# Near units of a block-sparse attention: key slots as row groups of the scores, squares turned on VectorE, sums from a column of ones

## The chip, the core and the metric

The kernel runs on one core of a Trainium2 chip. A core has five engines that work side by side: TensorE (PE, matrix products into PSUM), VectorE (DVE), ScalarE (ACT), GpSimd (POOL) and SyncE (SP, which here only issues transfers). The metric is the time of one execution in microseconds (us), the median of several runs.

## The reference

Two layers follow each other: a block-sparse attention and a channel mix.

```python
batch, n_heads, seq, head_dim = (4, 8, 768, 64); block = 32; n_rand = 3
mask = |blk_i - blk_j| <= 1  or  blk_i, blk_j in (0, 23)     # 24 blocks of 32 rows
mask[rows of qb, columns of kb] = True   for kb in sampled_blocks[qb]   # 3 drawn
scores = where(mask, q k^T / 8, -1e9)
attn = exp(scores - max); attn /= sum(attn) + 1e-9
x = (attn v), heads side by side                       # (4, 768, 512)

x_prev = x one row earlier (zeros ahead of row 0)
xk = mu_k x + (1 - mu_k) x_prev;  xr likewise with mu_r
out = sigmoid(xr w_r) * ((relu(xk w_k) ** 2) w_v)      # w_k 512x1024, w_v 1024x512, w_r 512x512
```

## The kernel before

The attention is cut into 24 units of 128 query rows, six for each batch b. Unit (b, 0) is a wide one: blocks 21, 22, 23 and 0, whose rows look at all or nearly all 24 blocks. The units (b, 1) to (b, 5) are near units: four blocks each (QB = 4), and each block looks at eight key slots of 32 keys: block 0, block 23, its own block and both neighbours, and three drawn blocks. `UNITS` puts the wide ones early: (0,0), (1,0), (2,0), (0,1), (0,2), (3,0), then the other near units in order.

A near unit is worked by `near_group`, twice, four heads at a time. Scores `s` are 16 products (L524) of 32 query rows by 256 keys, with a pair of heads in the two halves of the rows and the four blocks in the four column groups of the array, so the partitions of `s` are the query rows. VectorE adds the mask and takes the row's extreme in one operation a head (`soft`, L479); ScalarE takes the exponential with that as bias and sums the row into `L` (`exp`, L489); `turn` transposes 128x128 squares on PE into PSUM `t` (L500), and VectorE copies them back to `pt` (L506); 32 products of 64 columns with the values in VR make `o` (L546). `finish` divides `o` by `L` (L609), transposes the unit's `x` (`tx`, L606) and ScalarE puts it into `xt`, the input of the mixer.

The keys of a near unit lie in four buffers of KR (of five), one for each block with its eight slots: SP loads the three neighbours from kd, the ends once a batch, and the drawn blocks from kt, by numbers read from a register. The values of a block lie in one of six buffers VR: SP loads the known 128 rows (vw), GpSimd gathers the others by a list of rows (vt).

The channel mix goes by windows of 256 rows: `gate` (r, L713), `hidden` (h_0p to h_3p, L731) and `values` (v, L760), three products with numbers split in two parts for each product of the reference. A window needs the near units that cover its rows, so mixer and attention run side by side on PE; the windows of the last batch come after the attention.

All operations are first recorded by `Plan.add`, each with its engine, a cost in ns, a rank (its due time), what it reads and writes, and a release time. `Plan.order` then lists them engine by engine; what it lists is the program's order on each engine. The constants behind the functions (due times such as O_MAX and O_PV, lead times such as LEAD_K, M_STEP of the mixer, numbers of buffers) set this order. PSUM's eight banks stand as: `t` two, `m` (mixer) one, `o` one, `s` two of two banks each.

Of the kernel before, what the change touches and what calls it, by code (L numbers as in the profile page):

```python
# [18 lines left out]
P = 128  # L19
# [10 lines left out]
QB, NC, SLOTS = 4, 5, 8  # L30
# [185 lines left out]
def block_sparse_attention_channel_mix(  # L216
# [24 lines left out]
    KR = [fixed([P, SLOTS, HP * BLK], F32, f"KR{i}") for i in range(KR_BUFS)]  # L241
    VR = [fixed([P, 2, DM], F32, f"VR{i}") for i in range(VR_BUFS)]
    number = fixed([1, NB * NRAND * 2], I32, "number")
# [3 lines left out]
    near_mask = fixed([P, NC, SLOTS], F32, "near_mask")  # L247
# [6 lines left out]
    def mask_setup():  # L254
        own = buf([P, NC + 1, NRAND, 2], I32, "kk", 3, "own")
        con = buf([P, NC * (SEEN + SLOTS) + 2 * NB + 2], F32, "zr", 3, "con")
        pick = buf([P, NC * QB, 2], I32, "kk", 3, "pick")
        f = buf([P, NC + 1, NRAND], F32, "dif", 2, "ownf")
        same = buf([P, NB * NRAND], F32, "x0", 1, "same")
        word = buf([P, 2 * NB], F32, "x1", 1, "word")  # L260
        line = buf([P, NC * QB], F32, "pt", PT_BUFS, "line")
        near = NC * SEEN
        stat = near + NC * SLOTS
        plan.add(SP, ISSUE, -30, lambda: nc.sync.dma_start(number.ap, blocks), writes=[(number,)], size=2000)
        plan.add(ACT, ISSUE, -32, lambda: nc.scalar.dma_start(own.ap.rearrange("p a b c -> p (a b c)"), rows), writes=[(own,)], size=20000)
        plan.add(ACT, ISSUE, -31, lambda: nc.scalar.dma_start(con.ap, consts), writes=[(con,)], size=60000)
        plan.add(ACT, ISSUE, PICK, lambda: nc.scalar.dma_start(pick.ap.rearrange("p a b -> p (a b)"), picks), writes=[(pick,)], size=20000)
# [12 lines left out]
        def find():  # L280
            v = nc.gpsimd
            c = con.ap
            v.tensor_copy(out=line.ap, in_=pick.ap[:, :, 0])
# [8 lines left out]
        def far():  # L292
            v = nc.vector
            v.tensor_copy(out=f.ap, in_=own.ap[:, :, :, 0])
            c = con.ap

            e = same.ap.rearrange("p (a b) -> p a b", b=NRAND)
            v.tensor_tensor(
                out=e, in0=c[:, stat : stat + NB].unsqueeze(2).to_broadcast([P, NB, NRAND]),
                in1=f.ap[:, 0, :].unsqueeze(1).to_broadcast([P, NB, NRAND]), op=ALU.is_equal)  # L300
            v.tensor_reduce(out=wide_mask.ap, in_=e, axis=AX.X, op=ALU.max)
            v.tensor_tensor(out=wide_mask.ap, in0=wide_mask.ap, in1=c[:, stat + NB : stat + 2 * NB], op=ALU.max)
            v.tensor_scalar(out=wide_mask.ap, in0=wide_mask.ap, scalar1=1.0, scalar2=FAR, op0=ALU.subtract, op1=ALU.mult)

        def twice():
            v = nc.vector
            c = con.ap
            v.tensor_copy(out=near_mask.ap, in_=c[:, near:stat].rearrange("p (a b) -> p a b", b=SLOTS))
            g = f.ap[:, 1:, :]
            e = same.ap[:, 0 : NRAND * SEEN].rearrange("p (a b) -> p a b", b=SEEN)  # L310
            for a in range(NC):
                v.tensor_tensor(
                    out=e, in0=g[:, a, :].unsqueeze(2).to_broadcast([P, NRAND, SEEN]),
                    in1=c[:, a * SEEN : (a + 1) * SEEN].unsqueeze(1).to_broadcast([P, NRAND, SEEN]), op=ALU.is_equal)
                v.tensor_reduce(out=near_mask.ap[:, a, SEEN:], in_=e, axis=AX.X, op=ALU.max)
# [104 lines left out]
    def load_unit(b, u, at):  # L420
# [7 lines left out]
        if u == 0:  # L428
# [484 lines left out]
```

## Time and profile before

| what | value |
|---|---|
| timed runs | 616.49, 617.76, 619.31 us; median 617.76 |
| span of the profiled execution | 616.1 us (its time is given by this span alone) |
| PE, weight loads of PE | 575.8 us (93%), 465.5 us (76%) |
| DVE, ACT, POOL | 303.8 (49%), 300.6 (49%), 344.0 (56%) |
| transfers | 114.18 MB, mean 185 GB/s |

The span is that of the slowest core, of which there is one. PE's busy time is the time in which at least one product was in work; products overlap, and their ends are modelled, so in a list by time the distance from one start to the next tells more than the lengths. The rows that follow in the prediction are of three kinds: a table by stretch of time, a list of one engine by time, and groups by line of the kernel.

### The profile page before, as it was taken

The page shows a single profiled execution, that of the slowest core. Times are in us where ns is not written, and L with a number is a line of the kernel's source. Part 1 is how long each engine was busy: PE and PEld are TensorE (multiplying, and loading weights), DVE is VectorE, ACT ScalarE, POOL GpSimd, SP SyncE. Part 2 cuts the span into 40 slices and gives each one's busy share as a digit, 9 for nine tenths or more (in the row PEclk, how much of TensorE's full clock was granted, in tenths as well). Part 3 has the DMA queues.
Part 4 walks back from the last instruction along what each step waited for, and adds up shares of the span by engine and source line. Part 5 has one row for each costly group of instructions (what it writes and reads, how often), then busy time and mean ns, then how long its engine had stood idle before and what let it go on. Part 6 is the DMA issues. An engine that isn't in the chain of part 4 may idle for free.

```text
span 616.1 us, 20666 instructions
## 1 busy us (share of the span) xinstructions
PE 575.8 (93%) x8172; PEld 465.5 (76%) x8172; DVE 303.8 (49%) x906; ACT 300.6 (49%) x712; POOL 344.0 (56%) x400
## 2 busy tenths in 40 slices
PE   8887878798899999999999989999999999999997
PEld 3564655587667878878788778778778788989897
DVE  6677768873864255264443452653632532423300
ACT  3675845583544545355535534635545454333341
POOL 1324344865777737657836835546467464664551
PEclk9999989999899999999999999999999999999999
DMA  8959659858786667766764774774666620000001
GB/s 310 399 157 379 231 168 335 282 164 286 219 261 217 188 193 212 210 181 202 227 200 164 232 227 146 233 229 147 224 188 182 201 75 1 36 18 18 17 18 35
DMA packets 88499, 114.18 MB, mean 185 GB/s; under 512 B 12626, under 2 KB 59219, under 8 KB 88403
## 3 DMA queue, kind: packets, MB, share of 16 engines
q1 hardware_dynamic: 81570, 91.79, 46.7%
q0 software_dynamic: 6400, 20.98, 10.7%
q8 instruction: 65, 1.06, 0.7%
q10 hardware_dynamic: 432, 0.10, 0.2%
q14 instruction: 32, 0.25, 0.1%
HBM read 106.01 MB, written 6.82 MB: 183 GB/s over the span
## 4 chain that ended last, share of the span: by engine, by line
PE 63%; DVE 10%; ACT 8%; issue 6%; POOL 5%; DMA 3%; another core or an unknown queue 2%; SPq 2%; ACTq 0%; DVEq 0%; POOLq 0%
PE v L760 17%; PE o L546 5%; PE h_1p L731 5%; PE h_3p L731 5%; PE r_0p L713 5%; PE t L500 5%; PE r_1p L713 4%; PE h_2p L731 4%; ACT p L489 4%; PE s L524 3%; PE h_0p L731 2%; PE tw L500 2%; PE sw L563 2%; PE o L585 2%
## 5 line engine op out<-in xcount | busy, mean ns | idle before, releaser
L760 PE MATMUL v<-wv,k 128*128 128x512 f32 (+1 forms) x600 | 139.4, 386 | 1.4 <-DVE z L768 1.4
L760 PEld LDWEIGHTS v<-wv,k 128*128 128x128 f32 x600 | 107.5, 188 | 26.5 <-DVE xr_2f L680 2.1
L489 ACT ACTIVATE p<-p,nm 128x256 f32<-128x256 f32 x160 | 79.4, 498 | 48.7 <-DVE nm L479 48.7
L470 POOL DMA_INDIRECT VR<-vt,lines x80 | 79.0, 988 | 33.1 <-PE o L546 16.0
L506 DVE COPY pt<-t 128x512 f32<-128x512 f32 x80 | 53.0, 686 | 81.5 <-PE t L500 74.6
L479 DVE CUSTOM_DVE_ANT_1 p<-s,near_mask 128x256 f32<-128x256 f32 x160 | 57.9, 418 | 30.4 <-remote 19.4
L689 POOL TENSOR_TENSOR xr<-xr_1f,xr 128x256 fp32r<-128x256 f32 x24 | 17.7, 740 | 72.0 <-ACT xr L687 71.9
L524 PE MATMUL s<-KR,q 64*32 64x256 f32 x1280 | 50.8, 381 | 1.0 <-PE tw L500 0.9
L500 PE MATMUL t<-ident,p 128*128 128x128 f32 x320 | 47.5, 283 | 3.8 <-ACT p L489 2.3
L546 PEld LDWEIGHTS o<-VR,pt 128*32 128x32 f32 x2560 | 37.9, 110 | 15.0 <-issue 8.8
L546 PE MATMUL o<-VR,pt 128*32 128x64 f32 x2560 | 44.7, 221 | 2.3 <-issue 1.4
L687 ACT CAST xr<-xr_1f 128x256 fp32r<-128x256 f32 x24 | 9.7, 405 | 72.9 <-PE r_0p L713 43.0
L731 PE MATMUL h_1p<-xk,wk 128*128 128x256 f32 x288 | 37.0, 283 | 8.2 <-ACT h_0k L744 4.6
L609 DVE TENSOR_TENSOR x<-o,R 128x512 f32<-128x512 f32 x24 | 16.6, 691 | 56.8 <-PE o L546 53.7
L500 PEld LDWEIGHTS t<-ident,p 128*128 128x128 f32 x320 | 36.9, 144 | 9.3 <-ACT p L489 6.4
L731 PEld LDWEIGHTS h_1p<-xk,wk 128*128 128x128 f32 x288 | 34.7, 188 | 10.3 <-ACT h_0k L744 5.5
L731 PEld LDWEIGHTS h_0p<-xk,wk 128*128 128x128 f32 x288 | 34.9, 188 | 3.6 <-issue 3.3
L713 PE MATMUL r_1p<-wr,xr 128*128 128x512 f32 x144 | 37.7, 411 | 0.0
L524 PEld LDWEIGHTS s<-KR,q 64*32 64x32 f32 x1280 | 27.1, 105 | 13.8 <-issue 3.8
L731 PE MATMUL h_3p<-xk,wk 128*128 128x256 f32 x288 | 36.8, 282 | 0.4 <-ACT h_2k L744 0.4
L731 PEld LDWEIGHTS h_2p<-xk,wk 128*128 128x128 f32 x288 | 34.6, 188 | 3.3 <-ACT k L745 3.3
L731 PE MATMUL h_0p<-xk,wk 128*128 128x256 f32 x288 | 36.9, 283 | 0.0
(115 smaller groups left out, 1043.7 us busy)
## 6 DMA issues: line engine op xcount, KB each, us to landing
VR<-vw SPq DMA_DIRECT2D x80, 256.0 KB
KR<-kd SPq DMA_DIRECT2D x80, 192.0 KB
KR<-kt SPq DMA_DIRECT2D x240, 64.0 KB
k_ring<-kq SPq DMA_DIRECT2D x16, 384.0 KB
VR<-vt SPq DMA_DIRECT2D x24, 256.0 KB
q<-qt SPq DMA_DIRECT2D x23, 256.0 KB
out<-z SPq DMA_DIRECT2D x23, 256.0 KB
early_w<-w_k SPq DMA_DIRECT2D x8, 512.0 KB
```

The costliest lines, as they stand in the source:

```text
L470: plan.add(POOL, GATHER, at - LEAD_V + 0.01 * j, lambda w=w, n=n: nc.gpsimd.indirect_dma_start(VR[w].ap[:, 1, :], None, vt.rearrange("b n ...
L479: nc.vector.tensor_tensor_reduce(out=p.ap[:, cs].rearrange("p (a x) -> p a x", x=BLK), in0=view().rearrange("p (a x) -> p a x", x=BLK), in ...
L489: plan.add(ACT, 280 + 0.83 * (cs.stop - cs.start), rank, lambda: nc.scalar.activation(p.ap[:, cs], p.ap[:, cs], AF.Exp, bias=nm.ap[:, col ...
L500: nc.tensor.transpose(tp.ap[:, i, :], p.ap[:, cs], ident.ap)
L506: plan.add(DVE, 600, rank + 0.1, lambda: nc.vector.tensor_copy(out=pt.ap, in_=tp.ap), reads=[(tp,)], writes=[(pt,)])
L524: nc.tensor.matmul(s.ap[ROWS[j], row, a * 256 : (a + 1) * 256].rearrange("p (n x) -> p n x", x=BLK), q.ap[half, hp, ROWS[j]], KR[keys[j]]. ...
L546: nc.tensor.matmul(o.ap[ROWS[j], h * D : (h + 1) * D], pts[i // 2].ap[:, 2 * (i % 2) + g, ROWS[j]], VR[values[j]].ap[:, g, h * D : (h + 1) ...
L609: plan.add(DVE, 600, rank, lambda: nc.vector.tensor_tensor(out=x.ap.rearrange("p (h d) -> p h d", d=D), in0=o.ap.rearrange("p (h d) -> p h ...
L689: plan.add(POOL, 80 + 2.4 * MIX * tw, rank + O_MIX, lambda f=f, cs=cs: nc.gpsimd.tensor_tensor(out=dst.ap[:, 1, cs], in0=f.ap, in1=dst.ap[ ...
L713: nc.tensor.matmul(pr.ap[:, 0:512], xr.ap[:, a, c, :], wr.ap[:, w, c, :], start=(c == 0 and m == 0), stop=(c == CC - 1 and m == 2))
L731: nc.tensor.matmul(ph.ap[:, ff * TT : (ff + 1) * TT], wk.ap[:, w, c, f * P : (f + 1) * P], xk.ap[:, a, c, :], start=(c == 0 and m == 0), s ...
L760: nc.tensor.matmul(pv.ap[:, 0:width], k2.ap[:, a, f, i * P : (i + 1) * P], wv.ap[:, w, f, cs], start=(f == 0 and m == 0), stop=(f == FC - ...
```

## The change

`near_unit` takes the place of `near_group` and works all eight heads of a unit. The partitions of `s` were the 128 query rows; now row group i of `s` holds slot pair i for the 32 rows of a block, and the four blocks lie side by side in the columns: a product (L536) takes 32 query rows and the 64 keys of one slot pair. A row of queries so has its 256 scores on four partitions, 64 on each. The maximum is then taken in three steps: over 64 keys by VectorE (`tops`), from row group to row group by 16 products with parts of the unit matrix (`G`), over the four by VectorE again (`base`, with the penalty for slots that stand twice). VectorE subtracts (L567), ScalarE takes the exponential of 1024 columns without a sum, VectorE turns every 32x32 square in place (L572), and the products with the values read that directly: the key slots are already the rows. V has a 65th column of ones for each head, so the sum of a row comes out in `o`; `o` is two halves of one bank each, and `finish` divides each half for itself. PE's transposes of `p` go for near units; the wide units keep theirs.

KR becomes two buffers of a whole unit (6 neighbouring blocks, the two ends, 12 drawn). In PSUM, `t` and `m` become one tag of two banks, `o` gets two. The mask setup changes with it, and all of the planner's costs and due times have new numbers.

```diff
-QB, NC, SLOTS = 4, 5, 8
+QB, NC = 4, 5
+END, DRAWN = QB + 2, QB + 4
+KEYS = DRAWN + QB * NRAND
+DV = D + 1
+HD = H * DV
...
-    KR = [fixed([P, SLOTS, HP * BLK], F32, f"KR{i}") for i in range(KR_BUFS)]
-    VR = [fixed([P, 2, DM], F32, f"VR{i}") for i in range(VR_BUFS)]
+    KR = [fixed([P, KEYS, HP * BLK], F32, f"KR{i}") for i in range(KR_BUFS)]
+    VR = [fixed([P, 2, HD], F32, f"VR{i}") for i in range(VR_BUFS)]
...
+        plan.add(SP, ISSUE, at_k, lambda: nc.sync.dma_start(
+            KR[r].ap[:, 0:END].rearrange("p n x -> p (n x)"), kd[b, :, n0 - 1 : n0 + QB + 1].rearrange("p n x -> p (n x)")),
+            writes=[(KR[r], "near")], release=at_k, size=65536 * END)
...
                 for i in range(NRAND):
+                    nc.sync.dma_start(KR[r].ap[:, DRAWN + NRAND * j + i, :],
+                                      kt[bass.ds(sampled_block(n0 + j, i) + b * NB, 1)].rearrange("o p x -> p (o x)"))
...
-        tp = buf([P, 4, P], F32, "t", T_BUFS, f"t{name}", ps)
+        tp = buf([P, 4, P], F32, "m", M_BUFS, f"t{name}", ps)
...
+    def near_unit(b, u, q, keys, values, o, t0, gap):
...
+        G = buf([P, QB, 2 * C], F32, "m", M_BUFS, f"G{name}", ps)
+        for gi in range(2):
...
+            def mm(s=s, gi=gi):
+                for a in range(2):
+                    hp = 2 * gi + a
+                    for j in range(QB):
+                        for i in range(QB):
...
+                            for row, half in enumerate(HALF):
+                                at = (a * QB + j) * 2 * BLK
+                                nc.tensor.matmul(
+                                    s.ap[ROWS[i], row, at : at + 2 * BLK].rearrange("p (n x) -> p n x", x=BLK),
+                                    q.ap[half, hp, ROWS[j]], KR[keys].ap[half, near : far + 1 : far - near, hp * BLK : (hp + 1) * BLK],
+                                    start=True, stop=True, skip_group_check=True)
...
+            plan.add(DVE, N_TOP, t1 + O_MAX, lambda s=s, gi=gi: nc.vector.tensor_reduce(
+                out=tops.ap[:, gi * C : (gi + 1) * C], in_=s.ap.rearrange("p r (c x) -> p (r c) x", x=2 * BLK), axis=AX.X, op=ALU.max),
+                reads=[(s,)], writes=[(tops, gi)])
...
+        def spread():
+            for i in range(QB):
                 for j in range(QB):
+                    nc.tensor.matmul(G.ap[ROWS[j], i, :], ident.ap[:, ROWS[i]], tops.ap, start=True, stop=True, skip_group_check=True)
...
+        def top():
+            nc.vector.tensor_reduce(out=tops.ap, in_=G.ap.rearrange("p i c -> p c i"), axis=AX.X, op=ALU.max)
+            nc.vector.scalar_tensor_tensor(
+                out=base.ap.rearrange("p (h j) g -> p h j g", j=QB),
...
+                in1=near_pen.ap[:, (u - 1) * QB : u * QB, :].unsqueeze(1).to_broadcast([P, H, QB, 2]), op0=ALU.mult, op1=ALU.add)
...
+        for gi in range(2):
...
+            plan.add(DVE, N_SUB, t1 + O_MAX, lambda p=p, gi=gi: nc.vector.scalar_tensor_tensor(
...
+            plan.add(ACT, N_EXP, t1 + O_EXP, lambda p=p: nc.scalar.activation(p.ap, p.ap, AF.Exp), reads=[(p,)], writes=[(p,)], table="exp")
+            plan.add(DVE, N_TURN, t1 + O_TR, lambda p=p: nc.vector.transpose(p.ap, p.ap), reads=[(p,)], writes=[(p,)])
+
+            def pv(p=p, gi=gi):
...
+                                nc.tensor.matmul(
+                                    o[gi].ap[ROWS[j], i * DV : (i + 1) * DV], p.ap[:, at : at + BLK],
+                                    VR[values[j]].ap[:, g, h * DV : (h + 1) * DV], start=(g == 0), stop=(g == 1), skip_group_check=True)
...
+        for i in range(2):
+            each = slice(4 * i, 4 * i + 4)
...
+                nc.vector.tensor_scalar(out=r, in0=o[i].ap.rearrange("p (h d) -> p h d", d=DV)[:, :, D:DV], scalar1=1e-9, scalar2=None, op0=ALU.add)
+                nc.vector.reciprocal(r, r)
...
-            o = buf([P, DM], F32, "o", 1, f"o{b}_{u}", ps)
-            L = buf([P, H], F32, "L", 4, f"L{b}_{u}")
+            o = [buf([P, 4 * DV], F32, "o", 2, f"o{b}_{u}_{i}", ps) for i in range(2)]
...
-KR_BUFS, VR_BUFS, P_BUFS, PT_BUFS, T_BUFS, M_BUFS = 5, 6, 4, 4, 2, 1
+KR_BUFS, VR_BUFS, P_BUFS, PT_BUFS, M_BUFS = 2, 6, 4, 4, 2
...
-M_FIRST, M_STEP, M_LAST = 84.0, 41.265, 446.907
+M_FIRST, M_STEP, M_LAST = 85.515, 46.965, 816.505
```

What this does to the order is seen at three places. PE, batch 1's second window, while the hidden products run, before (unit (2, 2); names end in batch, unit and group):

```order
L524 MATMUL s2_2_0_5186<-KR2_71,q2_2_4914 32x256 x2
L731 MATMUL h1_1_0p_5210<-xk1_1_4840,wk_88 128x256 x24
L606 MATMUL tx2_1_5258<-ident_68,x2_1_5204 128x128 x4
L500 MATMUL t2_2_0_0_5266<-ident_68,p2_2_0_5225 128x128 x4
L731 MATMUL h1_1_1p_5274<-xk1_1_4840,wk_88 128x256 x24
L500 MATMUL t2_2_0_1_5306<-ident_68,p2_2_0_5225 128x128 x4
L524 MATMUL s2_2_1_5315<-KR4_73,q2_2_4914 32x256 x2
```

A group's scores, its two transposes and the next group's scores alternate with whole hidden products. PE at the same place after the change, the unit now being (2, 1):

```order
L536 MATMUL s2_1_0_5763<-KR0_69,q2_1_5384 32x64 x64
L536 MATMUL s2_1_1_5837<-KR0_69,q2_1_5384 32x64 x64
L651 MATMUL tx1_5_5907<-ident_68,x1_5_5722 128x128 x4
L752 MATMUL r1_1_0p_5915<-wr_85,xr1_0_2_5718 128x512 x12
L551 MATMUL G2_1_5932<-tops2_1_5904,ident_68 32x32 x16
L770 MATMUL h1_1_0p_5957<-xk1_1_5598,wk_84 128x256 x24
L770 MATMUL h1_1_1p_5990<-xk1_1_5598,wk_84 128x256 x12
L581 MATMUL o2_1_0_6010<-VR4_75,p2_1_0_5971 32x65
```

Both groups of scores now stand together, ahead of `tx` and a gate; the spread `G` follows, and one and a half hidden products stand between it and `o`.

VectorE for the same unit before:

```order
L479 ISA p2_2_0_5225,nm2_2_0_5226<-s2_2_0_5186,near_mask_83 128x256
L479 ISA nm2_2_0_5226 128x1
L680 SCALAR_TENSOR_TENSOR xk1_2f0_5256<-xk1_2d0_5251,mk_85,xt1_121 128x256
L680 SCALAR_TENSOR_TENSOR xk1_2f0_5256<-xk1_2d1_5254,mk_85,xt1_121 128x256
L506 COPY pt2_2_0_0_5287<-t2_2_0_0_5266 128x512
L506 COPY pt2_2_0_1_5332<-t2_2_0_1_5306 128x512
L479 ISA p2_2_1_5350,nm2_2_1_5351<-s2_2_1_5315,near_mask_83 128x256
```

One group's maxima, then copies of its transposes, with operations of the mixer between them. After the change, unit (2, 1):

```order
L542 TENSOR_REDUCE tops2_1_5904<-s2_1_0_5763 128x16
L542 TENSOR_REDUCE tops2_1_5904<-s2_1_1_5837 128x16
L556 TENSOR_REDUCE tops2_1_5904<-G2_1_5932 128x32
L557 SCALAR_TENSOR_TENSOR base2_1_5955<-tops2_1_5904,near_pen_79 128x64
L567 SCALAR_TENSOR_TENSOR p2_1_0_5971<-s2_1_0_5763,base2_1_5955 128x1024
L567 SCALAR_TENSOR_TENSOR p2_1_1_5985<-s2_1_1_5837,base2_1_5955 128x1024
L719 SCALAR_TENSOR_TENSOR xr1_1_1f1_5988<-xr1_1_1d2_5834,mk_81,xt1_117 128x128
L572 STREAM_TRANSPOSE p2_1_0_5971<-p2_1_0_5971 128x1024
L572 STREAM_TRANSPOSE p2_1_1_5985<-p2_1_1_5985 128x1024
```

Reductions, the base and both subtractions of the unit come first, one operation of the mixer stands between, and the two turns come last.

PE in the same window's values, after the change (unit (2, 2)):

```order
L752 MATMUL r1_1_1p_6325<-wr_85,xr1_1_1_5952 128x512 x6
L551 MATMUL G2_2_6355<-tops2_2_6322,ident_68 32x32 x16
L799 MATMUL v1_256_0_0_6382<-wv_2341,k21_1_6043 128x512 x24
L799 MATMUL v1_256_1_0_6427<-wv_2341,k21_1_6043 128x512 x3
L581 MATMUL o2_2_0_6435<-VR2_73,p2_2_0_6386 32x65
```

`G` stands behind the second gate and ahead of the values; `o` comes after 27 of the 48 products of the values.

More of the change, by code (lines that the diff above doesn't have):

```diff
@@ L500, in tr @@
                 nc.tensor.transpose(tp.ap[:, i, :], p.ap[:, cs], ident.ap)
-        plan.add(PE, 110 * len(parts), rank, tr, reads=[(ident,), *[(p, *keys) for p, keys, cs in parts]], writes=[(tp,)])
+        plan.add(PE, 128 * len(parts), rank, tr, reads=[(ident,), *[(p, *keys) for p, keys, cs in parts]], writes=[(tp,)])
         if act:
@@ L564, in mm @@
                                      start=True, stop=True)
-            plan.add(PE, 740, t0 + 0.1 * half_keys, mm, reads=[(q, hp), (K,)], writes=[(s,)], table="wide")
+            plan.add(PE, 820, t0 + 0.1 * half_keys, mm, reads=[(q, hp), (K,)], writes=[(s,)], table="wide")
             for row in range(2):
@@ L573, in wide_pair @@
             keys = [(row, 0), (2 + row, W)]
-            exp(ps_[row], slice(0, S), keys, nm, 2 + row, L, 2 * hp + row, t0 + O_EXP)
+            exp(ps_[row], slice(0, S), keys, nm, 2 + row, t0 + O_EXP)
             parts += [(ps_[row], keys, slice(n * P, (n + 1) * P)) for n in range(6)]
@@ L585, in pv @@
                         nc.tensor.matmul(
[L586 to L587 removed]
+                            o[h // 4].ap[ROWS[j], h % 4 * DV : (h % 4 + 1) * DV], pts[i // 4].ap[:, i % 4, ROWS[j]],
+                            VR[values[n // 2]].ap[:, n % 2, h * DV : (h + 1) * DV], start=(n == 0), stop=(n == 5),
                             skip_group_check=True)
[L590 to L591 removed]
@@ L593, in finish @@
-    def finish(b, u, o, parts, L, rank):
+            plan.add(PE, 820, t0 + O_PV + 0.05 * row, pv, reads=[(pts[i // 4],) for i in mine[::2]] + [(VR[w], 0, 1) for w in values],
+                     writes=[(o[h // 4], h % 4)], table="values")
+    def finish(b, u, o, parts, rank):
         x = buf([P, DM], F32, "pt", PT_BUFS, f"x{b}_{u}")
-        R = buf([P, H], F32, "L", 4, f"R{b}_{u}")
-        tp = buf([P, CC, P], F32, "t", T_BUFS, f"tx{b}_{u}", ps)
+        R = buf([P, H, 1], F32, "L", 4, f"R{b}_{u}")
+        tp = buf([P, CC, P], F32, "m", M_BUFS, f"tx{b}_{u}", ps)
@@ L866 @@
     row = np.repeat(of, BLK, axis=1).T
-    near = row[:, 1:, None]
-    seen = np.concatenate([0 * near, 0 * near + NB - 1, near - 1, near, near + 1], axis=2)
-    twice = np.zeros((P, NC, SLOTS))
-    twice[:, :, 0] = np.where(row[:, 1:] == 1, -FAR, 0.0)
+    mid = np.broadcast_to(np.arange(1, NB - 3)[None, :, None], (P, NC * QB, 1))
+    seen = np.concatenate([0 * mid, 0 * mid + NB - 1, mid - 1, mid, mid + 1], axis=2)
+    group = np.arange(P)[:, None] // BLK
+    twin = np.where((mid[:, :, 0] == 1) & (group == 0), FAR * SCALE, 0.0)
     blk = np.arange(NB)[None, :]
```

241 lines of the change are left out of this document (114 added, 127 removed).

## The prediction

> **What bounds the kernel now.** I read the busy time by stage first, then TensorE's own order of time inside one stage, then the groups of instructions by line for prices.
>
> ```profile
> 0.00:184.00 184.00, 156.34 (x3054) 111.20 (x3055) 130.11 (x364) 106.66 (x247) 93.30 (x116) 0.98 0.80 267
> 184.00:523.40 339.40, 330.01 (x4568) 274.02 (x4567) 150.11 (x479) 164.67 (x412) 204.45 (x239) 1.00 0.61 185
> 523.40:616.10 92.70, 89.49 (x555) 80.25 (x553) 23.62 (x65) 29.28 (x53) 46.23 (x46) 1.00 0.07 24
> ```
>
> A table by stretch: length, then busy time of PE, PEld, DVE, ACT and POOL, then granted clock, DMA share and GB/s. There are three stages. Up to 184 us the wide units, the weights and the first five near units run; PE is busy 156 of 184 us, DMA 0.80 of the time. From 184 to 523 us the fifteen other near units run between mixer windows, and PE is busy 330 of 339 us: this stage is bound by TensorE. The last 93 us are mixer alone, also on PE. The span ends at 616.1. The three timed runs have a median of 617.76, so 1.7 lies around the span or between executions; I make the sum against the span and add 1.7 at the end.
>
> One period of the middle stage, two near units and one mixer window, on PE (start, length, instructions; records of a product on a piece of the array come in twos):
>
> ```profile
> 314.88 3.05 PE L713 MATMUL r_0p<-wr,xr 128*128 128x512 f32 x12
> 317.86 1.10 PE L546 MATMUL o<-VR,pt 128*32 128x64 f32 x64
> 318.89 1.80 PE L524 MATMUL s<-KR,q 64*32 64x256 f32 x32
> 320.61 3.10 PE L731 MATMUL h_0p<-xk,wk 128*128 128x256 f32 x24
> 323.55 0.60 PE L606 MATMUL tx<-ident,x 128*128 128x128 f32 x4
> 323.98 0.60 PE L500 MATMUL t<-ident,p 128*128 128x128 f32 x4
> 325.45 3.00 PE L731 MATMUL h_1p<-xk,wk 128*128 128x256 f32 x24 [0.87 <-ACT h_0k L744]
> 328.29 0.60 PE L500 MATMUL t<-ident,p 128*128 128x128 f32 x4
> 328.82 1.09 PE L524 MATMUL s<-KR,q 64*32 64x256 f32 x32
> 329.84 3.10 PE L731 MATMUL h_2p<-xk,wk 128*128 128x256 f32 x24
> 332.87 1.10 PE L546 MATMUL o<-VR,pt 128*32 128x64 f32 x64
> 333.90 3.10 PE L731 MATMUL h_3p<-xk,wk 128*128 128x256 f32 x24
> 336.84 1.04 PE L500 MATMUL t<-ident,p 128*128 128x128 f32 x8
> 337.75 3.07 PE L713 MATMUL r_1p<-wr,xr 128*128 128x512 f32 x12
> 340.75 1.10 PE L546 MATMUL o<-VR,pt 128*32 128x64 f32 x64
> 341.78 5.76 PE L760 MATMUL v<-wv,k 128*128 128x512 f32 x24
> 347.38 0.60 PE L606 MATMUL tx<-ident,x 128*128 128x128 f32 x4
> 347.90 1.96 PE L524 MATMUL s<-KR,q 64*32 64x256 f32 x64
> 349.79 3.71 PE L760 MATMUL v<-wv,k 128*128 128x512 f32 x15
> 353.33 1.03 PE L500 MATMUL t<-ident,p 128*128 128x128 f32 x8
> 354.12 2.33 PE L760 MATMUL v<-wv,k 128*128 128x512 f32 x9
> 356.39 1.10 PE L546 MATMUL o<-VR,pt 128*32 128x64 f32 x64
> 357.42 1.09 PE L500 MATMUL t<-ident,p 128*128 128x128 f32 x8
> 358.27 0.71 PE L713 MATMUL r_0p<-wr,xr 128*128 128x512 f32 x2
> ```
>
> Instructions overlap, so I charge each row the time to the next row's start. The period is 358.27 - 314.88 = 43.39 us. The transposes `t` take 0.60 + 0.53 + 0.91 + 0.79 + 0.85 = 3.68, 1.84 a unit. The products `o` take 1.03 for one group of four heads, scores `s` 1.02 (0.95 in the pair), `tx` 0.48. Two waits are left: 0.87 ahead of h_1p, and 0.70 inside the first `s` (1.72 against 1.02). That is 0.78 a unit.
>
> **The change, part by part.** The 16 transposes of a unit go: -1.84.
>
> Scores: a group now has 64 products of 64 columns instead of 16 of 256, the same columns on the same eight pieces of the array (64 rows by 32 columns each). By columns a group stays at 0.95 to 1.02. By count the nearest row is `o`: 32 products, 64 records, in 1.03, so 32 ns a product, and 64 products would take 2.06. But is 32 ns a step between starts, or the columns of four pieces? A short stretch inside that `o` row, its records alone, tells:
>
> ```profile
> 317.86:317.88 0.02, 0.02 (x4) 0.02 (x4) 0.00 (x0) 1.00 0.69 256
> ```
>
> Four records of products start within 0.02 us, one on each piece: 5 to 7 ns apart. At 7 ns the 128 records of a group need 0.90, less than their columns. So `o` is held by its four pieces, the scores have eight, and I take 0 for the group, with +1.08 as the far end. [...]
>
> The new spread `G`: 16 products of 32 columns on four pieces, 32 records. Against `o` (64 records of 64 columns, 1.03) that is 0.26 by columns, 0.52 by count: I take 0.35. `o` with 65 columns for 64: +0.03 a unit. `tx` stays.
>
> Mixer products run slower just after attention's products. Alone they show:
>
> ```profile
> 534.78 2.83 PE h_1p L731 x24
> 543.26 2.80 PE r_1p L713 x12
> 546.06 10.90 PE v L760 x48
> ```
>
> A window alone is 2 x 2.80 + 4 x 2.83 + 10.90 = 27.8; in the period the same rows (2.98, 2.94, 2.84, 3.03, 2.94, 3.00, 5.60, 3.54, 2.27) make 29.1. So each of nine entries costs 0.15. In the new order there are seven: -0.15 a unit.
>
> PE work of a unit: -1.84 + 0.35 + 0.03 - 0.15 = -1.61.
>
> The waits. With two banks under `m`, h_1p no longer waits for h_0k, and `s` has its own wait gone; those 0.78 go. But a new chain stands between scores and `o`: G, VectorE's maximum and base, two subtractions, exp on ScalarE, the turn in squares, then `o`. Prices:
>
> ```profile
> L479 DVE CUSTOM_DVE_ANT_1 p<-s,near_mask 128x256 f32<-128x256 f32 x160 | 57.9, 418 | 30.4 <-remote 19.4 <-PE s L524 8.3 <-PE tx L606 2.7
> L479 DVE CUSTOM_DVE_ANT_1 pw<-sw,wide_mask 128x384 f32<-128x384 f32 x32 | 16.8, 552 | 1.7 <-PE sw L563 1.4
> L489 ACT ACTIVATE p<-p,nm 128x256 f32<-128x256 f32 x160 | 79.4, 498 | 48.7 <-DVE nm L479 48.7
> L489 ACT ACTIVATE pw<-pw,nmw 128x768 f32<-128x768 f32 x32 | 30.0, 938 | 11.8 <-DVE nmw L479 11.6
> L506 DVE COPY pt<-t 128x512 f32<-128x512 f32 x80 | 53.0, 686 | 81.5 <-PE t L500 74.6
> L808 ACT ACT_TABLE_LOAD x9 | 11.5, 1283 | 0.2
> L720 ACT COPY z<-r_1p 128x512 f32<-128x512 f32 x12 | 7.0, 584 | 20.8 <-PE r_1p L713 20.8
> ```
>
> ```profile
> 319.16 0.69 DVE L609 TENSOR_TENSOR x<-o,R 128x512 f32<-128x512 f32 x1 [3.15 <-PE o L546]
> ```
>
> From 418 and 552 ns a VectorE column costs 1.05 ns and an operation 0.15 us, so one of 1024 columns takes 1.22 us; so for the reduction, the subtraction and the turn, which no row shows. A dearer turn is the second rival's. [...] An exp of 1024 is 498 + 768 x 0.86 ns = 1.16 (0.86 from 498 and 938). An operation of 32 or 64 columns is 0.15 + 0.05 = 0.2. A hand-over between engines is 0.2: `o` ended at 318.96 in PE's list, VectorE began on it at 319.16.
>
> In the half with the hidden products, counted from the end of G: hand-over, maximum and base 0.66, subtractions done at 1.88 and 3.10, a mixer operation to 3.4, first turn 4.62, so `o` can start at 4.8. PE has h_0p and half of h_1p to do, 2.94 + 1.42 = 4.36: a wait of 0.46. The second group is ready at 6.0, the first ends at 5.9. I take 0.6 for this unit. In the half with the values, v waits for r_1p's bank (0.2 + 0.58 against G's 0.35: 0.43), and exp stands behind two table loads and the sigmoid: 0.78 + 1.28 + 1.2 + 1.28 = 4.5, turns end at 7.1 and 8.3; PE reaches `o` at 0.78 + 5.60 + 0.7 to 1.4: some 0.6 in all. So 0.6 a unit comes where 0.78 went. I take no change; ends -0.78 and +0.8.
>
> What else moves is covered. ScalarE drops from eight exp a unit to two; the row sums come from ones in V, so `L` and its read-outs go. SP's key loads are one near stretch and the drawn blocks, and with two whole-unit buffers a unit's keys are queued behind the scores of two units earlier, one unit, some 20 us, ahead of use. V rows grow from 2048 to 2080 bytes, near keys halve; with DMA at 0.61 neither shows. VectorE gets dearer by 6 x 1.22 + 0.4 less (57.9 + 53.0)/20: 2.2 a unit, and has room in the middle stage, 150 of 339.
>
> Middle stage: 15 x -1.61 = -24.2. Last stage: nothing. First stage: five units are worth 5 x 1.61 = 8 if PE were the bound, but there:
>
> ```profile
> 100.00:120.00 20.00, 14.90 (x290) 10.39 (x288) 18.35 (x39) 10.77 (x24) 13.88 (x15) 1.00 0.93 303
> ```
>
> VectorE at 18.35 of 20 us and DMA at 0.93 bind, and if VectorE bound throughout, five units would cost 5 x 2.2 = 11. I take the middle of -8 and +11: +1.5.
>
> Sum: 616.1 - 24.2 + 1.5 = 593.4 for the span, 595.1 with what lies around it; I say 595.
>
> **Rivals.**
> Scores run by a step for each product, not by columns: at the 32 ns of `o` +1.08 a group, +2.16 a unit, against -1.61: +0.55, over 20 units +11, so 629, slower. It decides from a score group above 1.8 us. For it: 128 loads of weights and 128 records stand in a stretch that has 32 of each now, and no row shows products under 32 ns for longer than a burst of four. Against it: the 5 to 7 ns within that burst. Chance 0.14, of which 0.04 for a step near 28 ns, which gives 1.8 a group and leaves the time within 0.5%. [...]
>
> The chain on VectorE is longer than PE's cover: if its 1024-column operations take 1.6 us rather than 1.22, two subtractions and a turn add 1.1 to each unit's wait, 15 x 1.1 = 17: 612. From 1.6 more wait a unit nothing is left of the gain. For it: both subtractions stand ahead of the first turn, and `o` waits for all of them. Against it: the 512 columns of `x` above took 0.69, just what 0.15 + 512 x 1.05 ns gives, so the price holds at twice the length. Chance 0.17, a third of that within 0.5%.
>
> The waits vanish altogether and the first stage gains in full: 595 - 15 x 0.78 - 9.5 = 574. Chance 0.12. For it: 0.6 a unit rests on mixer operations of VectorE that may fall elsewhere.
>
> Key loads come late and eat the gain, no measurable change: 0.02; two buffers would have to cost 1.6 a unit where SP had 20 us.
>
> **How the numbers follow.** The forecast of about 595 (585 to 605 with its own bounds) has 0.55. The range 577 to 613 takes in the waits at +0.8 (12 us) or the first stage at +11 above, and the waits at -0.78 with part of the first stage below; outside are the scores by product, the long end of VectorE's chain and the far end of the third rival. About 0.5% is what a measurement of this kernel tells from no change, 614.7 to 620.8 here: faster 0.55 + 0.12 + 0.11, same 0.04 + 0.06 + 0.02, slower 0.10.
>
> **What would show it.** Groups of scores at 0.95 to 1.05 us in PE's order of time, `G` at 0.35, no `t` of near units; periods of about 40.2 us instead of 43.4; turn, subtraction and reduction near 1.2 us each; waits of PE on the turn of 0.6 a unit. It is wrong if a group of scores takes over 1.3, if PE waits over 1.5 a unit on VectorE, or if the middle stage starts later than 190.

## The result, and the profile after

The changed kernel takes 693.45 us (median of four runs, 689.09 to 699.19) where the kernel before takes 617.65 on the same chip: 1.123 times, 95% interval 1.117 to 1.129. The forecast was 595. The profiled execution has a span of 686.1 us; the busy times on its page:

```profile
PE 589.6 (86%) x12332; PEld 488.0 (71%) x12332; DVE 375.6 (55%) x728; ACT 260.9 (38%) x402; POOL 348.9 (51%) x400
```

PE has 12332 records of products where it had 8172, and the span is 70 us longer with only 14 us more of busy PE (589.6 against 575.8): the rest is PE standing idle. The table by stretch, cut where the second and the tenth mixer window begin, as the prediction's was:

```profile
0.00:197.00 197.00, 158.34 (x4028) 117.12 (x4028) 137.58 (x307) 91.06 (x141) 93.12 (x109) 0.91 0.71 238
197.00:599.08 402.08, 347.47 (x7786) 295.13 (x7777) 210.32 (x362) 140.74 (x209) 212.76 (x252) 0.94 0.47 142
599.08:686.10 87.02, 83.78 (x531) 75.77 (x529) 27.74 (x60) 29.14 (x52) 43.02 (x41) 0.99 0.06 22
```

The middle stage took 339.4 and was 97% busy; now it takes 402 and PE idles 55 of them, and the granted clock (the number after the five engines) is 0.94 instead of 1.00. The first stage is 13 us longer. The last is 6 shorter, since 24 products of the window before it now stand ahead of it.

PE by time in the middle stage, two pairs of groups of scores:

```profile
339.06 2.33 PE L536 MATMUL s<-KR,q 64*32 64x64 f32 x215
343.63 0.90 PE L536 MATMUL s<-KR,q 64*32 64x64 f32 x41 [2.23 <-issue]
344.47 1.11 PE L651 MATMUL tx<-ident,x 128*128 128x128 f32 x4
345.23 3.85 PE L752 MATMUL r_0p<-wr,xr 128*128 128x512 f32 x12
349.01 0.46 PE L551 MATMUL G<-tops,ident 128*32 128x32 f32 x32
...
363.40 2.17 PE L536 MATMUL s<-KR,q 64*32 64x64 f32 x197
367.94 0.81 PE L536 MATMUL s<-KR,q 64*32 64x64 f32 x59 [2.37 <-issue]
368.68 1.66 PE L752 MATMUL r_1p<-wr,xr 128*128 128x512 f32 x6
```

A pair of groups, forecast at 1.9 to 2.0 us, takes 344.47 - 339.06 = 5.41 and 368.68 - 363.40 = 5.28. Inside each there is a hole of over 2 us, and the releaser is named "issue": PE waits for nothing that the profile shows, no semaphore, no engine. Behind the first hole `tx` takes 0.76 where it took 0.48, and the gate `r_0p` 3.78 where it took 2.98. The clock tells why (length, busy PE, then the granted clock, DMA share and GB/s, in the stretch from 344.40 and in the one behind it):

```profile
344.40:349.70 5.30, 5.07 (x54) 0.75 0.68 241
349.70:365.00 15.30, 15.24 (x388) 1.00 0.45 136
```

Behind this hole the clock is lowered for a while, so it costs twice. That isn't so of every hole: the one of 2.37 us is followed by a clock of 1.00 from 368.70 to 374.00.

By groups of instructions, the scores of the kernel before first, then the changed kernel:

```profile
L524 PE MATMUL s<-KR,q 64*32 64x256 f32 x1280 | 50.8, 381 | 1.0 <-PE tw L500 0.9
L536 PE MATMUL s<-KR,q 64*32 64x64 f32 x5120 | 74.7, 237 | 57.8 <-issue 55.2
L542 DVE TENSOR_REDUCE tops<-s 128x16 f32<-128x1024 f32 x40 | 48.8, 1220 | 102.0 <-PE s L536 92.2
L567 DVE SCALAR_TENSOR_TENSOR p<-s,base 128x1024 f32<-128x1024 f32 x40 | 47.1, 1217 | 0.6
L572 DVE STREAM_TRANSPOSE p<-p 128x1024 f32<-128x1024 f32 x40 | 47.7, 1222 | 5.7 <-ACT p L571 5.5
L752 PE MATMUL r_0p<-wr,xr 128*128 128x512 f32 x144 | 45.1, 471 | 2.5 <-issue 2.5
```

The scores hold PE for 74.7 busy and 57.8 idle, 132.5 us; before it was 50.8 and 1.0. VectorE's three large operations take 1.22 us each, exactly as forecast. VectorE waits 92.2 us for the scores; PE waits 2.6 us for VectorE ahead of them.

### The profile page after: what moved, and what is told of

It reads as the page before. It is cut to its first block, busy times and chain, and to the rows that moved or that the text cites. A ratio compares the mean times of both kernels' runs of the same rounds, so it can differ in the third digit from the quotient of the medians.

```text
span 686.1 us, 28239 instructions
## 1 busy us (share of the span) xinstructions
PE 589.6 (86%) x12332; PEld 488.0 (71%) x12332; DVE 375.6 (55%) x728; ACT 260.9 (38%) x402; POOL 348.9 (51%) x400
## 4 chain that ended last, share of the span: by engine, by line
PE 79%; issue 11%; DVE 7%; ACT 2%; POOL 0%; DVEq 0%; ACTq 0%; POOLq 0%
PE v L799 20%; PE s L536 10%; PE o L581 6%; PE r_0p L752 6%; PE h_0p L770 5%; PE r_1p L752 5%; PE h_2p L770 5%; PE h_1p L770 5%; PE h_3p L770 5%; PE o L620 3%; PE tw L503 3%; PE sw L598 2%; PE tx L651 2%; DVE wmag L372 1%; DVE pw L482 1%
## 5 line engine op out<-in xcount | busy, mean ns | idle before, releaser
L536 PE MATMUL s<-KR,q 64*32 64x64 f32 x5120 | 74.7, 237 | 57.8 <-issue 55.2
L536 PEld LDWEIGHTS s<-KR,q 64*32 64x32 f32 x5120 | 60.6, 110 | 70.6 <-issue 65.9
L542 DVE TENSOR_REDUCE tops<-s 128x16 f32<-128x1024 f32 x40 | 48.8, 1220 | 102.0 <-PE s L536 92.2
L572 DVE STREAM_TRANSPOSE p<-p 128x1024 f32<-128x1024 f32 x40 | 47.7, 1222 | 5.7 <-ACT p L571 5.5
L571 ACT ACTIVATE p<-p 128x1024 f32<-128x1024 f32 x40 | 42.0, 1059 | 22.3 <-DVE p L567 21.3
L581 PEld LDWEIGHTS o<-VR,p 128*32 128x32 f32 x2560 | 39.3, 112 | 13.1 <-issue 8.3
L581 PE MATMUL o<-VR,p 128*32 128x65 f32 x2560 | 43.9, 224 | 4.9 <-issue 4.9
L567 DVE SCALAR_TENSOR_TENSOR p<-s,base 128x1024 f32<-128x1024 f32 x40 | 47.1, 1217 | 0.6
L752 PE MATMUL r_0p<-wr,xr 128*128 128x512 f32 x144 | 45.1, 471 | 2.5 <-issue 2.5
L752 PEld LDWEIGHTS r_0p<-wr,xr 128*128 128x128 f32 x144 | 32.9, 236 | 10.4 <-issue 3.0
```

Of the source, the lines that this page charges most:

```text
L536: nc.tensor.matmul(s.ap[ROWS[i], row, at : at + 2 * BLK].rearrange("p (n x) -> p n x", x=BLK), q.ap[half, hp, ROWS[j]], KR[keys].ap[half, ...
L542: plan.add(DVE, N_TOP, t1 + O_MAX, lambda s=s, gi=gi: nc.vector.tensor_reduce(out=tops.ap[:, gi * C : (gi + 1) * C], in_=s.ap.rearrange("p ...
L567: plan.add(DVE, N_SUB, t1 + O_MAX, lambda p=p, gi=gi: nc.vector.scalar_tensor_tensor(out=p.ap.rearrange("p (c x) -> p c x", x=BLK), in0=ss ...
L571: plan.add(ACT, N_EXP, t1 + O_EXP, lambda p=p: nc.scalar.activation(p.ap, p.ap, AF.Exp), reads=[(p,)], writes=[(p,)], table="exp")
L572: plan.add(DVE, N_TURN, t1 + O_TR, lambda p=p: nc.vector.transpose(p.ap, p.ap), reads=[(p,)], writes=[(p,)])
L581: nc.tensor.matmul(o[gi].ap[ROWS[j], i * DV : (i + 1) * DV], p.ap[:, at : at + BLK], VR[values[j]].ap[:, g, h * DV : (h + 1) * DV], start= ...
```

## The experiments

They ran on a chip on which the kernel before takes 603 to 608 us, so ratios to it are compared, not times (the changed kernel's 1.123 stems from the first chip); where an expectation gives a time, it is against 617.7.

Two theories stood against each other. The supply theory: PE carries out instructions faster than they are brought to it. A product of fp32 on a piece of the array is two products and two weight loads in the stream (`s` has 5120 records for 40 groups of 64 products, and PE as many weight loads as records, 12332), so a unit's scores are 512 instructions: 64 products a group, two groups, four instructions each. The step theory, which is the first rival of the prediction: each small product costs a fixed time on PE itself. A third, that the new chain through VectorE costs the time, was already unlikely from the rows above, and the second trial was to decide it.

**The cut alone, in the kernel before.**

```diff
-                for j in range(QB):
-                    for row, half in enumerate(HALF):
-                        nc.tensor.matmul(s.ap[ROWS[j], row, a * 256 : (a + 1) * 256]...
+                for c in range(4):
+                    for j in range(QB):
+                        for row, half in enumerate(HALF):
+                            at = a * 256 + c * 64
+                            nc.tensor.matmul(s.ap[ROWS[j], row, at : at + 64]...
```

> The kernel before, with each product of the scores over 256 columns cut into four of 64 (64 products a group for 16, the same columns, everything else as before). Supply theory (PE runs dry because a burst of small products eats its fetched instructions faster than they are brought, and faster still while GpSimd runs an indirect DMA): a group that stands between mixer products stays near 1.0 to 1.5 us, the pairs of groups in the values half take 4 to 7 us with idle time inside them; 635 to 665 us, the loss lying in the pairs and in gaps beside GpSimd's indirect DMAs. Step theory (a small product needs a fixed time of its own on PE, about 32 ns): every group takes about 2.06 us, alike everywhere, without long gaps; 617.7 + 40 x 1.08 = 661 us.

Measured: 1.114 times the time before (1.107 to 1.120; 675.58 against 605.4). So this one part of the change, put alone into the kernel before, costs nearly all that the whole change costs, and more than either theory gave it (665 of 617.7 is 1.077). PE in the values half, where two groups stand together, and the group of the scores:

```profile
334.10 3.37 PE L526 MATMUL s<-KR,q 64*32 64x64 f32 x254
340.20 0.30 PE L526 MATMUL s<-KR,q 64*32 64x64 f32 x2 [2.73 <-issue]
...
L526 PE MATMUL s<-KR,q 64*32 64x64 f32 x5120 | 73.6, 231 | 36.5 <-issue 34.9 <-PE tw L500 0.9 <-DMA KR<-kd 0.5
```

Holes of "issue" again, 34.9 us in 17 waits. The pair shown takes 340.42 - 334.10 = 6.3 us (its next row starts at 340.42), inside the 4 to 7 of the supply theory. The step theory has no place for the hole: 254 records pass in 3.4 us, and then the last two come 2.7 later. These products read neighbouring slots as in the kernel before, so the changed kernel's way of picking slot pairs isn't what costs.

**The changed kernel without the cut.** A group's scores are 16 products of 256 columns. They leave out the choice of slots and take eight that lie side by side, so the scores' values don't hold; all else stays.

```diff
-                    for j in range(QB):
-                        for i in range(QB):
...
-                                    s.ap[ROWS[i], row, at : at + 2 * BLK]..., q.ap[half, hp, ROWS[j]], ...
+                    for i in range(QB):
+                        for row, half in enumerate(HALF):
+                            nc.tensor.matmul(
+                                s.ap[ROWS[i], row, a * 256 : (a + 1) * 256]..., q.ap[half, hp, ROWS[i]],
+                                KR[keys].ap[half, 2 * i : 2 * i + 8, ...]
```

> The changed kernel, with a group's scores as 16 products of 256 columns, which take the key slots in the wrong arrangement (the scores' values are left wrong; columns, tiles, all other operations and the order stay). Supply theory and step theory: the burst is gone, a group takes about 1.0 us, no gap over 0.4 us inside the scores, PE's clock stays at 1.0 behind them, and the rest of the prediction shows: 590 to 612 us. Chain theory (the new chain through VectorE and ScalarE costs the time, not the scores): PE waits ahead of o instead, and the time stays above 660 us.

Measured: 0.970 (0.966 to 0.974; 587.34 against 605.4). Groups and stretches:

```profile
L533 PE MATMUL s<-KR,q 64*32 64x256 f32 x1280 | 41.2, 386 | 1.7 <-DVE p L564 1.6
L749 PE MATMUL r_0p<-wr,xr 128*128 128x512 f32 x144 | 36.0, 399 | 0.0
...
0.00:179.81 179.81, 151.00 (x3069) 106.78 (x3069) 137.65 (x308) 91.10 (x141) 92.95 (x110) 0.93 0.76 257
179.81:499.24 319.43, 308.95 (x4905) 257.27 (x4897) 210.81 (x362) 140.82 (x209) 212.61 (x251) 0.99 0.59 180
```

The chain theory falls: the chain is all there, and the kernel is faster than before. Between this kernel and the changed one the span differs by 99.8 us (586.3 and 686.1, on two chips), and it lies in the scores for the most part: they have 42.9 busy and idle against 132.5, 89.6 more, of which 56.1 are idle and 33.5 busy. `r_0p` has 36.0 against 47.6, 11.6 more, of which 2.5 are a hole and the rest goes with the lowered clock behind holes, as above; smaller differences both ways nearly cancel. Half a period on PE, from behind the `G` of the half with the hidden products to behind `o`:

```profile
302.00 3.09 PE L767 MATMUL h_0p<-xk,wk 128*128 128x256 f32 x24 [0.29 <-ACT z L756]
304.93 1.57 PE L767 MATMUL h_1p<-xk,wk 128*128 128x256 f32 x12
306.44 2.02 PE L578 MATMUL o<-VR,p 128*32 128x65 f32 x128
308.39 1.68 PE L767 MATMUL h_1p<-xk,wk 128*128 128x256 f32 x12
```

`o` starts without a wait here.

**No indirect DMAs.** In the changed kernel, most short gaps lie beside GpSimd's gathers (a fence on them is in the last section), so these were replaced:

```diff
-            plan.add(POOL, GATHER, ..., lambda w=w, n=n: nc.gpsimd.indirect_dma_start(
-                VR[w].ap[:, 1, :], None, vt..., bass.IndirectOffsetOnAxis(ap=lines.ap[:, b, n - 1 : n], axis=0)), ...
+            plan.add(SP, ISSUE, ..., lambda w=w, n=n: nc.sync.dma_start(VR[w].ap[:, 1, :], vw[b, n - 1]), ...
```

> The changed kernel, with GpSimd's 80 indirect DMAs for the drawn values replaced by plain loads from SyncE of as many bytes (the drawn values are left out; the others are loaded twice). Supply theory: the 51 short gaps of 0.5 to 0.7 us inside the scores and o, 28 us together, all of which lie beside an indirect DMA, go; the gaps of 1.3 us and over, at every 256th instruction, stay: 660 to 675 us. Step theory: indirect DMAs have nothing to do with PE's pace; 685 to 695 us.

Measured: 1.121 (1.116 to 1.127; 680.1 against 605.4), no different from the changed kernel's 1.123. The time went the step theory's way, but the trace doesn't: the waits of the scores on "issue", sum, times and longest, without the gathers, and in the changed kernel:

```profile
PE s L534 <- issue: 59.6, 25, 4.8
```

```profile
PE s L536 <- issue: 55.2, 56, 4.6
```

Most of the short gaps went, as said (56 waits became 25), and the long ones grew by as much. So the gathers don't set the time; with them PE only spends some of the same wait earlier.

**The scores in smaller bursts.** The same instructions in another order, twice: eight operations of 16 products a unit, and four of 32 (each N_S / 2, due from t0 on, 4 us apart), among the mixer's products.

```diff
-            plan.add(PE, N_S, t1, mm, ..., writes=[(s,)], table="scores")
+            every = [(a, j) for a in range(2) for j in range(QB)]
+            for part in range(4):                       # 2 in the second kernel
+                mine = every[part * 2 : (part + 1) * 2]   # 4
+                plan.add(PE, N_S / 4, t0 - 8 + 2 * (4 * gi + part), lambda mine=mine, mm=mm: mm(mine), ..., writes=[(s, part)], table="whole")
```

> The changed kernel, with the scores of a unit recorded as eight operations of 16 products (instead of two of 64), due 2 us after each other from 8 us earlier on, so that they alternate with halves of the mixer's products; the same products and instructions. Supply theory: fewer than 100 instructions a microsecond are asked of any stretch, gaps inside the scores sink from 4 us a unit to below 1; eight to twelve more entries of 0.15 us a unit take part of it back: 625 to 650 us. Step theory: the same products take the same time wherever they stand, and the entries come on top: 690 to 715 us.

> The changed kernel with a unit's scores as four operations of 32 products, due 4 us after each other, so that they stand between whole mixer products: fewer entries than the eight operations of the earlier trial, longer bursts. Supply theory: a burst of 128 instructions in 0.6 us and a hidden product of 48 in 2.9 us is 50 instructions a microsecond, less than the 73 at which blocks came in the changed kernel (256 in 3.5 us), so gaps in the scores stay near those of the eight operations (35 to 40 us in all, most of them in the first stage), and some 10 us of entries are saved: 1.05 to 1.08 of the time before. Step theory: 1.12 or more.

Measured: 1.085 (1.080 to 1.090; 656.41 against 605.4) and 1.080 (1.076 to 1.085; 652.83 against 604.59). The scores of the first kernel, then a wait and the scores of the second:

```profile
L536 PE MATMUL s<-KR,q 64*32 64x64 f32 x5120 | 75.4, 230 | 30.7 <-issue 24.4 <-DVE p L570 3.3 <-DVE nmw L482 3.0
```

```profile
PE G L554 <- DVE tops L545: 20.1, 13, 3.0
L536 PE MATMUL s<-KR,q 64*32 64x64 f32 x5120 | 73.2, 231 | 14.4 <-issue 11.0 <-DVE p L570 2.3 <-PE tx L654 0.9
```

Moved apart, the very same products wait 24 or 11 us for instructions instead of 55, which no fixed step explains; but the time is short of what I expected: for the eight operations 650 of 617.7 at most, 1.05, and for the four just the upper end, 1.08, though only 11 us of gaps are left where I expected 35 to 40. The scores' busy time has hardly moved: 75.4 and 73.2 us, where 16 products a group have 41.2. That part of the loss goes with the small products wherever they stand, as a step would; the next section asks how much of it is a step. And part of what is saved is spent elsewhere. In the second kernel the last piece of scores stands right ahead of `G`, and `G` now waits 20 us for VectorE. In the first, every piece interrupts the mixer:

```profile
310.53 0.45 PE L536 MATMUL s<-KR,q 64*32 64x64 f32 x32
310.91 1.69 PE L773 MATMUL h_2p<-xk,wk 128*128 128x256 f32 x12
312.53 0.45 PE L536 MATMUL s<-KR,q 64*32 64x64 f32 x32
```

Half a hidden product takes 1.62 here, where half of the 2.83 of a window alone is 1.42: 0.2 for each entry, of which I count sixteen a period. Neither order beats the kernel before.

**Half the cut.** 32 products of 128 columns a group, again without the choice of slots.

```diff
+                    for c in range(2):
+                        ... s.ap[ROWS[i], row, at : at + 128]..., q.ap[half, hp, ROWS[i]],
+                            KR[keys].ap[half, 2 * i + 4 * c : 2 * i + 4 * c + 4, ...]
```

> Between the changed kernel and the one with 16 products a group: 32 products of 128 columns a group (the key slots again in the wrong arrangement; all columns, tiles and other operations stay). Supply theory: a unit's scores are now 256 instructions, one block of the instruction fetches, in 2 us, and mixer products of 16 instructions a microsecond follow, so the fetch keeps up: gaps over 0.4 us in the scores under 5 us in all, 0.965 to 0.985 of the time before, close to the 0.970 of 16 products. A loss by the count of instructions, wherever they stand: a third of the way from 0.970 to 1.123, 1.02. Step theory at 32 ns a product: 1.02 us a group, as at 16.

Measured: 0.987 (0.978 to 0.997); the runs spread from 593.4 to 602.4, against 604.59. That is 0.002 above the expected stretch, whose upper end the interval includes; 1.02 is excluded. The scores' wait on "issue":

```profile
PE s L535 <- issue: 0.2, 1, 0.2
```

Of the two doublings from 16 to 64 products the first costs some 0.017 and the second 0.136. So the loss doesn't grow in proportion to the number of products. This trial can't tell the two theories apart, though: a step of 32 ns is hidden behind the columns of 32 products and not of 64, so it too would show only at the second doubling.

**The pace by itself.** Bursts of small products that nothing uses, in the kernel before, at its start and behind its end (one run, of which the trace is read and not the time).

```diff
+                        nc.tensor.matmul(w.ap[i * BLK : (i + 1) * BLK, row, at : at + 64], src[half, i * BLK : (i + 1) * BLK],
+                                         src[half, 0:64], start=True, stop=True, skip_group_check=True)
...
+    burst("f0", "f", 32, -19)        # 256 products of fp32
+    burst("h0", "h", 64, -18)        # 512 of bf16
+    burst("f1", "f", 32, 5000, 3000)
+    burst("h1", "h", 64, 5001, 3000)
```

> The kernel before, with bursts of small products that nothing uses added at both ends: ahead of the first scores, and again behind the last product of the mixer, where the transfers are quiet, 256 fp32 products of 64 columns on the scores' eight pieces (four fetched instructions each, as two records and two weight loads) and then 512 bf16 products of 64 columns (two instructions each). Both bursts are 1024 instructions, four blocks. Supply theory: both take the same time, set by the blocks, 2.5 to 3.5 us for 256 instructions behind the first one or two blocks, 8 to 13 us a burst, with gaps once in 256 instructions, though bf16 does twice the products; the start's bursts take longer than the end's, since the transfers are busy there. Step theory (32 ns a product): 8 us for fp32 and 16 us for bf16, evenly, at both ends. By columns alone 3.6 us for fp32.

PE behind the kernel's end, the fp32 burst (bf) and then the bf16 burst (bh), and the transfers of the same stretch (packets, MB, share of the engines):

```profile
636.26 2.72 PE L825 MATMUL bf<-ident 64*32 64x64 f32 x255
641.18 1.47 PE L825 MATMUL bf<-ident 64*32 64x64 f32 x128 [2.21 <-issue]
644.93 2.04 PE L825 MATMUL bf<-ident 64*32 64x64 f32 x128 [2.28 <-issue]
648.67 0.31 PE L825 MATMUL bf<-ident 64*32 64x64 f32 x1 [1.71 <-issue]
648.68 1.36 PE L825 MATMUL bh<-const-bfloat16-1.0 64*32 64x64 bf16 x127
652.14 1.28 PE L825 MATMUL bh<-const-bfloat16-1.0 64*32 64x64 bf16 x128 [2.11 <-issue]
655.89 1.28 PE L825 MATMUL bh<-const-bfloat16-1.0 64*32 64x64 bf16 x128 [2.47 <-issue]
659.63 1.28 PE L825 MATMUL bh<-const-bfloat16-1.0 64*32 64x64 bf16 x128 [2.47 <-issue]
663.38 0.23 PE L825 MATMUL bh<-const-bfloat16-1.0 64*32 64x64 bf16 x1 [2.46 <-issue]
...
q8 instruction: 6, 0.10, 1.9%
```

This settles that there is a supply limit. The first 255 records, two blocks, pass in one go. From then on there are 128 records to a block (the blocks that begin at 648.67 and 663.38 open with one record of the burst before and with the last record), with their weight loads 256 instructions, and the blocks start 3.75, 3.74, 3.47, 3.75, 3.74 and 3.75 us apart, for fp32 and bf16 alike, though a block of fp32 is 64 products and one of bf16 128. The records are carried out within 1.3 to 2.0 us; then PE waits until the next block. How fast PE runs the records isn't the reason: the block at 641.18 took it 1.47 us and the one at 644.93 2.04, and the distance to the next is the same, 3.75 and 3.74. That is a bit more than the 2.5 to 3.5 that I expected. The fp32 burst takes 12.7 us, since its first two blocks were there, and the bf16 burst 14.9, not 8 to 13; the step theory's 16 is near that by chance, since its products would come evenly.

In 24 us, six packets of 16 KB (0.10 MB) move on the instruction queue, and no other bytes. On the pages of the two kernels this queue has 65 packets before and 96 after the change; twice the records of PE (a weight load each), 16344 and 24664, are about 64 and 96 times 256. So PE's instructions came in blocks of 256, by the packets' size 64 bytes each, and behind the kernel's end, where nothing else moved, one in 3.47 to 3.75 us. The six packets take 1.9% of 16 engines in these 24 us, some 1.2 us each by this estimate; what fills the rest of the 3.75 isn't shown.

The same blocks show in the kernels themselves. Counted through the changed kernel's trace in all of PE's records (12332 products, as many weight loads, 110 others, mostly for semaphores), 25 of its 26 holes of over 1 us that end on "issue" stand at the same place of 256 (193 or 194 past a multiple); so do 22 of 23 in the kernel before with the cut alone.

Behind the kernel's end a block took PE 1.3 to 2.0 us, less than the 3.75 to the next, and 1.7 to 2.5 us a block stand in the open. At the start, where transfers run (the page of the kernel before has 310 and 399 GB/s in its first two slices of 15.4 us), blocks stood as much as 6.2 us apart:

```profile
19.25 2.04 PE L825 MATMUL bf<-ident 64*32 64x64 f32 x128 [2.79 <-issue]
25.44 0.98 PE L825 MATMUL bf<-ident 64*32 64x64 f32 x51 [4.16 <-issue]
```

## Why the prediction was wrong, point by point

The step that failed is the one on the scores: "At 7 ns the 128 records of a group need 0.90, less than their columns", from four records that started within 0.02 us. Those four are far too few to show what a long burst is held by. A group's 128 records and 128 weight loads are as many instructions as a block, and behind the first two, blocks stood 3.47 to 3.75 us apart in the bursts at the kernel's end. In the changed kernel the scores took (74.7 + 57.8)/20 = 6.6 us a unit, not 2.0: 92.5 us more over 20 units, of which the forecast gain of 22.7 pays a part. What is left, 69.8, is the 70.0 by which the span grew; that it fits so closely is in part luck, since the lowered clock behind some holes is not in it and was made up for elsewhere.

The forecast's 7 ns were too low for PE itself as well. At the end of the kernel with the bursts, 255 fp32 records that had no hole took 2.72 us, the last one's length of some 0.2 included: 10 ns each, so 1.3 us for a group, an estimate from that row. A group of the changed kernel into which no hole falls, with the clock at 1.00:

```profile
154.75 1.48 PE L536 MATMUL s<-KR,q 64*32 64x64 f32 x128 [1.61 <-DVE p L567]
156.16 1.06 PE L770 MATMUL h_2p<-xk,wk 128*128 128x256 f32 x7
```

It takes 1.41 us against the 0.95 to 1.02 that I took. So 0.3 to 0.4 a group, 12 to 16 us over 40 groups by this estimate, would be left if no hole were. The rest of the 33.5 us of busy time by which the scores exceed those of the kernel without the cut isn't taken apart.

The first rival had the right place, the right sign and the deciding point (1.8 us a group). Its mechanism, a price for each product, holds in this smaller part, at some 20 ns rather than 32; that alone gives neither the sign nor 693, and the rival itself came to 629. The greater part is the holes: they stand at one place of 256 instructions, they shrink when the same products are put in another order, and in the bursts blocks come at one distance for 64 and for 128 products. Nor does a step between starts make them: in the bursts 128 bf16 products, each on one of eight pieces, pass within 1.28 us, 10 ns each, and then PE waits 2.1 to 2.5 us.

The remark in that rival, "128 loads of weights and 128 records stand in a stretch that has 32 of each now", was the decisive one. I weighed it by PE's own pace and never asked where the instructions come from, though the page of before lists an instruction queue. The kernel before even has such holes: its `o` of the wide units, small products too, waits 5.4 us on "issue" in five waits of up to 2.4, and its three holes of over 1 us in `o` all stand at 193 past a multiple of 256.

The other steps held, as the kernel without the cut shows: 0.970 measured where the forecast was 595 of 617.76, 0.963. It ran on the second chip, so its times below agree with the forecast's only as far as the chips do.

- Transposes gone, spread and 65 columns: `G` stands 0.38 us ahead of the next product in the kernel with scores in operations of 32 products (296.50 and 296.88; 0.35 forecast), and without the cut a pair of `o` takes 1.95 (forecast two times 1.03 and 0.03 more).
- VectorE's large operations: 1.22 us forecast, 1.217 to 1.222 measured; the turn, which no row of before showed, is no dearer. ScalarE's exp was 1.06 in the changed kernel, not 1.16.
- The chain: I expected 0.6 us of waiting a unit ahead of `o`. In the half period shown there is none; all of `o`'s waits on the turn in that kernel are 2.8 us, in six. The second rival falls.
- The waits that were to go went, and others came: seven ahead of `h_0p`, 2.0 us in all, and six ahead of `v`, 4.9, one of them 3.6.
- A period: 40.2 forecast. The gates that open two windows of the kernel without the cut stand 298.32 - 258.33 = 39.99 apart:

```profile
258.33 0.48 PE L749 MATMUL r_0p<-wr,xr 128*128 128x512 f32 x1
```

```profile
298.32 0.48 PE L749 MATMUL r_0p<-wr,xr 128*128 128x512 f32 x1
```

- The first stage, put at +1.5 for VectorE's sake, was 13 us longer in the changed kernel. Without the cut it is 17 shorter than that (179.81 against 197.00), so most of it was the scores again. Whether VectorE binds part of it, as I took, stays open: in the kernel without the cut it is busy 19.2 of the 20 us from 140 to 160, PE 14.5, and two of PE's three waits there, 1.9 and 1.6 us, are for VectorE.

## What to carry to other kernels

Count the instructions of a stretch, not only its columns: products and weight loads, twice for fp32 on a piece of the array. Here PE got 256 of them in 3.75 us, some 68 a microsecond, with nothing else moving, and at the kernel's start, among other transfers, as few as 256 in 6.2 us. At the most two blocks passed without a hole in the bursts, 255 records in 2.72 us; what stood behind them ran dry, though it was on the same eight pieces of the array. Going from 16 products of 256 columns to 32 of 128 cost some 1.7% of the time before, and on to 64 of 64 another 13.6%. A hole with "issue" as its releaser, at distances of 256 instructions, is the mark to look for; a clock below 1.00 behind it can be a second.

## What the runs showed of the hardware that I had not expected

The pace of 256 instructions in 3.75 us, with six instruction packets in 24 us, is told above. Beside it, PE's stream slowed to a trickle while GpSimd issued indirect DMAs. A stretch of the changed kernel, other engines left out:

```profile
540.42 0.71 PE L536 MATMUL s<-KR,q 64*32 64x64 f32 x46
...
540.81 0.96 POOL L473 DMA_INDIRECT VR<-vt,lines  x1 [0.38 <-issue]
...
541.36 0.33 PE L536 MATMUL s<-KR,q 64*32 64x64 f32 x4 [0.24 <-issue]
...
542.10 0.31 PE L536 MATMUL s<-KR,q 64*32 64x64 f32 x5 [0.41 <-issue]
```

Once the DMA_INDIRECT is on, a handful of records passes in about 0.1 us and then none for 0.6. Counted through the trace, 42 of the 49 waits on "issue" of under 1.3 us inside scores and `o` lie within 0.3 us of an indirect DMA: most, not all as the expectation had it. Without the gathers 7 such waits are left. In this kernel that cost nothing on top, since the blocks were late anyway. A gather alone doesn't do it: the two kernels with smaller bursts run the same 80, 78 us of them, and have only 23 and 17 waits on "issue" of any length in scores and `o`, where this one has 65. What else it takes, and what the two engines share, isn't shown.

And PE's clock fell behind one hole of some 2 us: 0.75 granted over the 5.3 us behind the one of 2.23, a gate of 12 products at 3.78 us instead of 2.98; behind the one of 2.37 it stayed at 1.00.
